# Attention output product for two heads' pairs at a time every second step, split a step later, and twenty narrower products of zeros

## The chip, the cores and the metric

The kernel runs on one core of a Trainium2 chip. The metric is the device time of one execution in microseconds (us). Engines are TensorE (PE, with its weight loads as PEld), VectorE (DVE), ScalarE (ACT), GpSimd (POOL) and SyncE (SP, which issues DMAs). Matmuls write into PSUM, eight banks of 512 fp32 columns by 128 partitions.

## The reference

Talking-heads attention (the heads are mixed before and after the softmax), then a dense gated MLP, then a routed mixture of experts. The change touches the attention alone:

```
batch, heads, seq, dim = 2, 12, 448, 64
scores = scale * q @ k.T                              # per batch and head
scores = einsum('bhij,hg->bgij', scores, w_pre)       # heads mixed
attn   = softmax(scores)
attn   = einsum('bhij,hg->bgij', attn, w_post)        # heads mixed again
x      = attn @ v                                     # -> [batch*seq, heads*dim]
x      = (x @ w_a) * (x @ w_b) @ w_out                # first MoE part, dense
out    = routed experts of x (8 experts, top 1)
```

All is fp32; the first dense product takes x as a sum of a rounded high part and a rest (hi and lo, `xh` and `xl`).

## The kernel before

The queries are cut into blocks of 120, 120, 120 and 90 per batch, eight blocks in all. A block is worked off in steps: `self.seq` lists 46 steps, n = 0 to 45, six for a block of 120 queries and five for one of 90. The order on every engine is the order of the code, written out by hand as a software pipeline in `Attention.run`. In step n TensorE does, in this order:

- `postmix` of step n - 1 into the two PSUM banks o (L165): the attention weights mixed over heads, transposed by the matmul. The exponentials `e` are the stationary operand.
- `qk_mm` (L90): the scores of one pair of heads of a later block, into the two banks s. The last are done in step 36.
- `premix` of step n + 2 (L122): the scores mixed over heads, into banks of the pool t. It has three banks; a step takes two, one for each r.
- `av` (L189): the output product attn @ v of the block before, one sixth of it (two heads, `p` = 0 to 5) at a time, into the single bank v. A sixth of a block of 120 takes 120 columns of the bank.

ScalarE has in a step: the exponentials of step n + 1 (L139), one half of the copy of o into `A2T` (L177), one half of the score copy into `S` (L96), and the high part of the output product, `xh` (L206). VectorE has the other half of the copy of o (L177), the normaliser (L147, L148), the other half of the score copy (L97), the row maxima of step n + 2 (L130), and the low part `xl`, which is the product minus its high part (L207). GpSimd scales the post-mix weights (L151) and issues most of the DMAs that rearrange the scores from `S` to `G` for `premix` (L111).

Sixths of a block become due in the second step of the block behind it. Before, a step takes one sixth, or two if there are more sixths left than steps. Of the last block all six sixths come behind the loop, in banks s and o. In the last steps a hook adds work: VectorE decodes weights for the dense part from step 39 on (L372 to L376), ScalarE and VectorE split them in step 42 (L392, L393), and steps 44 to 46 each end with six dense products (L414) behind everything else on TensorE.

Ahead of all this TensorE multiplies zeros (L233) while the first loads are under way.

Of the kernel before, what the change touches and what calls it, by code (L numbers as in the profile page):

```python
# [27 lines left out]
HP = H // 2  # L28
# [5 lines left out]
class Attention:  # L34
# [174 lines left out]
    def run(self, hook=None):  # L209
        nc = self.nc  # L210
        nb, N = len(self.blocks), len(self.seq)
        first = {}
        for n, s in enumerate(self.seq):
            first.setdefault(s[0], n)
        first[nb] = N
        AH, LAG, PRE = 5, 1, 5
        self.on_sp = [n < 10 or n - 1 in first.values() or n in first.values() for n in range(N)]
        c = self.c
        cs = self.att.tile([128, 4, 64], F32, name="cs")
        self.load_q(0)  # L220
        for p in range(HP):
            self.load_k(0, p)
        self.load_q(1)
        nc.sync.dma_start(cs, self.a["wmix"])
        nc.sync.dma_start(self.kc, self.a["kc"])
        self.load_v(0, 0)
        self.load_v(0, 1)
        z = self.att.tile([128, 2, S], F32, name="e", bufs=3)
        nc.vector.memset(z[:, 0, 0:256], 0.0)
        z = z[:, 0, 0:256].bitcast(BF16)  # L230
        zp = self.pair("t")
        for i in range(14):
            nc.tensor.matmul(zp[i % 2][:, :360], z[:, 0:128], z[:, :360], start=True, stop=True)  # L233
        nc.gpsimd.tensor_tensor(out=c["wpre"], in0=cs[:, 0], in1=cs[:, 1], op=ALU.mult)
        nc.gpsimd.tensor_scalar(out=c["wpre"], in0=c["wpre"], scalar1=0.125, scalar2=None, op0=ALU.mult)
        nc.gpsimd.tensor_tensor(out=c["wpost"], in0=cs[:, 2, 0:GK], in1=cs[:, 3, 0:GK], op=ALU.mult)
        for p in range(HP):
            self.qk_pair(0, p, ("s", "o", "tt", "tv")[p % 4])
        todo = [(blk, p) for blk in range(1, nb) for p in range(HP)]
        nrel = [0]  # L240
        def rel(n):
            while nrel[0] < min(n, N, first[todo[0][0]] if todo else N):
                self.relayout(nrel[0])
                nrel[0] += 1
        rel(2)
        self.load_q(2)
        rel(AH)
        for i in range(PRE):
            self.qk_pair(*todo.pop(0), "so"[i % 2])
        for m in range(2):  # L250
            self.premix(m)
            self.rowmax(m)
        self.exps(0)
        self.norm(0)
        loads = {}
        for i in range(HP):
            if i > 1:
                loads[i - 1] = lambda i=i: self.load_v(0, i)
            loads[9 + i] = lambda i=i: self.load_k(1, i)
            loads[(20, 22, 26, 27, 28, 29)[i]] = lambda i=i: self.load_v(1, i, True)  # L260
        parts = []
        for n in range(N + LAG):
            av, k = [], 0
            m = n - LAG
            if n < N:
                blk, g0, nr, last = self.seq[n]
                if n - 1 in first.values() and blk > 0:
                    parts = [(blk - 1, p) for p in range(HP)]
                left = (first[blk + 1] if blk + 1 < nb else N - 1) - n + 1
                av = [parts.pop(0) for _ in range(min(len(parts), 2 if len(parts) > left else 1))]  # L270
                if todo:
                    tb = todo[0][0]
                    need = sum(1 for x in todo if x[0] == tb)
                    if tb < 2 or n > first[tb - 1] - AH:
                        slots = first[tb] - AH - n + 1
                        k = min(need, 2 if need > slots else 1)
            if m >= 0:
                self.postmix(m)
            out = []
            for _ in range(k):  # L280
                for f in out:
                    f()
                out = [self.qk_mm(*todo.pop(0))]
            if n + 2 < N:
                self.premix(n + 2)
            if n + 1 < N:
                self.exps(n + 1)
            if m >= 0:
                self.a2t(m, 0)
                self.a2t(m, 1)  # L290
            if n + 1 < N:
                self.norm(n + 1)
            for f in out:
                f()
            pso = [(*av[0], len(av), self.av(*av[0], len(av)))] if av else []
            if n + 2 < N:
                self.rowmax(n + 2)
            for x in pso:
                self.av_out(*x)
            rel(n + 1 + AH)  # L300
            if n < N:
                for tb in range(3, nb):
                    if n == first[tb - 2] - 3:
                        self.load_q(tb)
                loads.get(n, lambda: None)()
            if not todo and not self.qk_closed:
                self.qk_es.close()
                self.qk_closed = True
            if self.qk_closed and nrel[0] == N and not self.s_closed:
                self.s_es.close()  # L310
                self.s_closed = True
            if hook:
                hook(n)
        self.last = nb - 1
# [1020 lines left out]
```

## Time and profile before

| | us |
|---|---|
| median of 3 runs | 627.27 |
| lowest and highest of them | 626.29, 630.08 |
| the profiled execution | 626.63 |
| its span, first to last instruction | 624.9 |
| TensorE busy with matmuls in it | 598.6 |
| VectorE busy | 416.1 |
| ScalarE busy | 234.0 |
| GpSimd busy | 143.4 |

The profile shows one execution. Its span is 1.73 us shorter than its time; what lies around the span is not seen. The attention loop runs to about 188 us of it; the dense part and the routed experts follow. Matmuls overlap, and the end of one is modelled, so the starts of TensorE's groups tell more than their busy time.

### The profile page before, as it was taken

How to read it: one execution, taken by the hardware profiler on the slowest of the kernel's cores; microseconds unless marked ns; L12 is line 12 of the kernel's file. 1: busy time of each engine (PE TensorE's matmuls, PEld its weight loads, DVE VectorE, ACT ScalarE, POOL GpSimd, SP SyncE). 2: the span in 40 equal slices, each digit the busy share in tenths (PEclk: the TensorE clock that was granted, in tenths of full speed). 3: DMA queues.
4: the chain of work that ended last, by engine and by line, in shares of the span. 5: the costliest groups of instructions: out<-in, count | busy, mean ns of one | idle time of the engine just before them, and what ended most of it. 6: DMA issues, size and time to landing. Idle time of an engine off the chain costs nothing. (4 is left out here: it accounts for less than half of the span.)

```text
span 624.9 us, 16865 instructions
## 1 busy us (share of the span) xinstructions
PE 598.6 (96%) x6843; PEld 497.7 (80%) x6843; DVE 416.1 (67%) x993; ACT 234.0 (37%) x544; POOL 143.4 (23%) x243
## 2 busy tenths in 40 slices
PE   8789999999999999999999999999999999979993
PEld 3346666666778999999999979999998888769982
DVE  4478787878856878777777555987759833593322
ACT  4376676766652211111111252212364222361221
POOL 3477666767700000000000015000100101101101
PEclk9799999999999999999999999999999999979998
DMA  7677638656322654444455003310490661156102
GB/s 225 177 193 189 187 114 206 177 180 171 119 64 72 231 188 167 152 152 160 171 178 201 0 1 116 140 50 26 175 335 1 252 254 53 48 225 259 48 31 66
DMA packets 38178, 89.89 MB, mean 144 GB/s; under 512 B 12208, under 2 KB 15596, under 8 KB 38076
## 3 DMA queue, kind: packets, MB, share of 16 engines
q1 hardware_dynamic: 24060, 64.60, 30.7%
q0 software_dynamic: 14016, 23.95, 13.0%
q8 instruction: 62, 1.02, 0.7%
q14 instruction: 40, 0.33, 0.2%
HBM read 69.88 MB, written 5.70 MB: 121 GB/s over the span
## 5 line engine op out<-in xcount | busy, mean ns | idle before, releaser
L111 POOL DMA_DIRECT2D G<-S x156 | 92.2, 609 | 18.9 <-issue 7.8
L1131 PE MATMUL y<-ra,gh 128*128 128x384 f32 x324 | 70.6, 340 | 0.0
L392 ACT CAST whi<-wdec 128x768 fp32r<-128x768 f32 x24 | 20.0, 835 | 124.2 <-DVE wdec L376 116.9
L139 ACT ACTIVATE e<-t,st 124x448 f32<-124x448 f32 x90 | 56.2, 633 | 15.1 <-DVE st L130 15.1
L838 PE MATMUL ph<-ra,xsh 128*128 128x512 f32 x168 | 54.9, 409 | 5.0 <-ACT ra L801 4.5
L130 DVE TENSOR_REDUCE st<-t 124x1 f32<-124x448 f32 x90 | 52.1, 619 | 11.2 <-PE t L122 8.4
L165 PEld LDWEIGHTS o<-Wp,e 60*56 60x56 f32 (+1 forms) x2880 | 48.2, 132 | 13.7 <-issue 12.5
L1131 PEld LDWEIGHTS y<-ra,gh 128*128 128x128 f32 x324 | 56.8, 188 | 0.6 <-issue 0.3
L122 PE MATMUL t<-G,wpre 60*64 60x448 f32 x360 | 53.4, 555 | 3.9 <-DMA G<-S 3.6
L165 PE MATMUL o<-Wp,e 60*56 60x60 f32 (+1 forms) x2880 | 54.0, 221 | 2.4 <-issue 1.4
L189 PEld LDWEIGHTS v<-A2T,vt 120*64 120x64 f32 x672 | 33.6, 136 | 26.6 <-DVE st L148 18.3
L1107 POOL TENSOR_TENSOR ra<-wo,ra 128x768 fp32r<-128x768 f32 x4 | 10.6, 2673 | 191.5 <-ACT ra L1106 191.5
L915 PE MATMUL py<-ra,gh 128*128 128x384 f32 x224 | 49.2, 342 | 0.0
L90 PE MATMUL s<-Kt,Q 64*64 64x448 f32 (+2 forms) x336 | 45.6, 551 | 0.6 <-ACT S L96 0.6
L807 POOL DMA_INDIRECT fa<-yd,idc x11 | 11.5, 1049 | 145.1 <-DVEq L874 64.3
L189 PE MATMUL v<-A2T,vt 120*64 120x120 f32 (+1 forms) x672 | 42.3, 269 | 0.2 <-DVE xl L207 0.2
L177 DVE COPY A2T<-o 120x480 f32<-120x480 f32 (+1 forms) x46 | 30.9, 671 | 16.0 <-PE o L165 15.8
L1131 PE MATMUL y<-ra,gl 128*128 128x384 f32 x162 | 41.3, 336 | 0.0
L838 PEld LDWEIGHTS ph<-ra,xsh 128*128 128x128 f32 x168 | 31.8, 195 | 11.6 <-ACT ra L801 4.9
L915 PEld LDWEIGHTS py<-ra,gh 128*128 128x128 f32 x224 | 38.8, 188 | 1.0 <-issue 1.0
L393 DVE TENSOR_TENSOR wlo<-wdec,whi 128x768 fp32r<-128x768 f32 x24 | 23.0, 958 | 22.4 <-ACT whi L392 22.3
L122 PEld LDWEIGHTS t<-G,wpre 60*64 60x64 f32 x360 | 20.6, 136 | 20.9 <-issue 6.4
(248 smaller groups left out, 1236.2 us busy)
## 6 DMA issues: line engine op xcount, KB each, us to landing
wraw<-in_wab_dram SPq DMA_DIRECT2D x48, 384.0 KB
G<-S POOLq DMA_DIRECT2D x156, 105.0 KB, 3.9
fa<-in_w_dram SPq DMA_DIRECT2D x4, 3072.0 KB
wor<-in_w_out_dram SPq DMA_DIRECT2D x12, 768.0 KB
r1f<-in_w_dram SPq DMA_DIRECT2D x2, 3072.0 KB
r1f<-in_wg_dram SPq DMA_DIRECT2D x8, 384.0 KB
r1f<-in_w_dram SPq DMA_DIRECT2D x4, 768.0 KB
fa<-in_w_dram SPq DMA_DIRECT2D x4, 768.0 KB
```

The lines of the kernel that those rows point to most:

```text
L90: nc.tensor.matmul(ps[r][64 * h:64 * h + m, :S], q[64 * r:64 * r + 64, p * 2 * hw + h * hw:p * 2 * hw + h * hw + m], k[64 * r:64 * r + 64, ...
L111: (self.nc.sync if r == 0 and (h == 0 and self.on_sp[n] or n < 2) else self.nc.gpsimd).dma_start(g[64 * r:64 * r + GK, h, :], self.S[blk][ ...
L122: nc.tensor.matmul(t[r][64 * h:64 * h + 64, :S], w[64 * r:64 * r + GK, :], g[64 * r:64 * r + GK, h, :], start=True, stop=True)
L130: self.nc.vector.tensor_reduce(out=st[:124, r:r + 1], in_=self.T[n][r][:124, :S], op=ALU.max, axis=AX.X, negate=True)
L139: self.nc.scalar.activation(e[:124, r, :], t[r][:124, :S], AF.Exp, bias=st[:124, r:r + 1], scale=1.0, accum_out=st[:124, 2 + r:3 + r])
L165: nc.tensor.matmul(o[h][64 * u:64 * u + m, c0:c0 + GK], e[64 * h:64 * h + GK, r, x:x + m], wp[64 * h:64 * h + GK, r, :], start=True, stop= ...
L177: (nc.scalar.copy if h == 0 else nc.vector.tensor_copy)(dst, src)
L189: nc.tensor.matmul(ps[u * 64:(u + 1) * 64, i * w:(i + 1) * w], self.vt[b, p][:, j, u, :], at[:, j * H + 2 * p + u, :w], start=(j == 0), st ...
L393: lambda: V.tensor_tensor(out=lo, in0=x3, in1=hi.bitcast(F32), op=ALU.subtract)]
L838: nc.tensor.matmul(ps, x[:, d], self.w1[:, hf, s, d], start=(d == 0 and i == 0), stop=(d == ND - 1 and i == 2))
L915: nc.tensor.matmul(y[q][:, :384], hx[:, f % 4], self.w2[:, f, s, q * 384:(q + 1) * 384], start=(f == 0 and i == 0), stop=(f == NFC - 1 and ...
L1131: nc.tensor.matmul(y[q][:, :384], gx[:, f % 6], wov[:, f, s, 384 * q:384 * (q + 1)], start=(t > 0 and f == 0 and i == 0), stop=(f == NF - ...
```

## The change

The sixths of a block go two by two into one bank, in the first, third and fifth of the steps in which one went before; the step between has no output product. The high and low part of such a pair are made in the step behind it, after that step's row maxima, except where another output product comes at once: then they are made ahead of that product. That happens twice: at step 24, since the block before has five steps, and at step 45, where the last two sixths are taken because it is the loop's last step; there its own pair is split at once too. Ahead of the loop, 14 products of zeros with 360 columns become 20 with 255.

```diff
-        for i in range(14):
-            nc.tensor.matmul(zp[i % 2][:, :360], z[:, 0:128], z[:, :360], start=True, stop=True)
+        for i in range(20):
+            nc.tensor.matmul(zp[i % 2][:, :255], z[:, 0:128], z[:, :255], start=True, stop=True)
...
-        parts = []
+        parts, pso = [], []
         for n in range(N + LAG):
...
                 if n - 1 in first.values() and blk > 0:
-                    parts = [(blk - 1, p) for p in range(HP)]
-                left = (first[blk + 1] if blk + 1 < nb else N - 1) - n + 1
-                av = [parts.pop(0) for _ in range(min(len(parts), 2 if len(parts) > left else 1))]
+                    parts, at = [(blk - 1, p) for p in range(HP)], n
+                if parts and ((n - at) % 2 == 0 or n == N - 1):
+                    av = [parts.pop(0) for _ in range(2)]
...
-            pso = [(*av[0], len(av), self.av(*av[0], len(av)))] if av else []
+            if av:
+                for x in pso:
+                    self.av_out(*x)
+                pso = []
+            done, pso = pso, ([(*av[0], len(av), self.av(*av[0], len(av)))] if av else [])
             if n + 2 < N:
                 self.rowmax(n + 2)
-            for x in pso:
+            for x in done + (pso if n >= N - 1 else []):
                 self.av_out(*x)
+            if n >= N - 1:
+                pso = []
```

On TensorE, at steps 7 and 8, where the output product of the first block begins (v is its bank, t that of the pre-mix, o that of the post-mix, s that of the scores; x8 are the eight matmuls of a sixth):

```order
 L90 MATMUL s<-Kt,Q 60x448
 L122 MATMUL t<-G,wpre 64x448 x4
-L189 MATMUL v<-A2T,vt 64x120 x8
+L189 MATMUL v<-A2T,vt 64x120 x16
 L165 MATMUL o<-Wp,e 64x60
 L165 MATMUL o<-Wp,e 56x60 x2
```

```order
 L90 MATMUL s<-Kt,Q 45x448
 L122 MATMUL t<-G,wpre 64x448 x4
-L189 MATMUL v<-A2T,vt 64x120 x8
 L165 MATMUL o<-Wp,e 64x60
 L165 MATMUL o<-Wp,e 56x60 x2
```

The second sixth has moved from step 8 into the group of step 7, and in step 8 the post-mix follows the pre-mix directly.

On ScalarE, from the copy of the weights of step 42 to the end of the loop (e are exponentials, A2T the copy of o, xh the high part). Before:

```order
L392 CAST whi_3263<-wdec 128x768
L139 ACTIVATE e,st<-t,st 124x448 x2
L177 COPY A2T<-o 120x2x48x5
L206 CAST xh<-v 128x2x12x10
L139 ACTIVATE e,st<-t,st 124x448
L177 COPY A2T<-o 120x2x48x5
L206 CAST xh<-v 128x12x10
L177 COPY A2T<-o 120x2x48x5
L206 CAST xh<-v 128x12x10
L177 COPY A2T<-o 120x48x5
```

Now:

```order
L398 CAST whi_3221<-wdec 128x768
L139 ACTIVATE e,st<-t,st 124x448 x2
L177 COPY A2T<-o 120x2x48x5
L206 CAST xh<-v 128x2x12x10
L139 ACTIVATE e,st<-t,st 124x448
L177 COPY A2T<-o 120x2x48x5 x2
L206 CAST xh<-v 128x2x12x10 x2
L177 COPY A2T<-o 120x48x5
```

The high part of the pair of step 44, the first of the two in the row with x2, now stands behind step 45's copy of o, and ahead of the high part of step 45's own pair.

## Rows read from the trace of the kernel before

**Rows 1.** Windows, three stretches of the loop: start:end, length, busy of each engine (instructions), clock, DMA

```profile
46.55:152.65 106.10, 105.34 (x2772) 70.34 (x2772) 85.08 (x205) 71.79 (x202) 73.69 (x145) 1.00 0.64 176
152.65:175.09 22.44, 22.44 (x642) 15.93 (x641) 19.54 (x47) 14.69 (x43) 14.79 (x27) 1.00 0.34 112
175.09:187.99 12.90, 12.68 (x311) 10.13 (x310) 6.14 (x14) 6.57 (x15) 0.67 (x2) 1.00 0.21 66
```

**Rows 2.** Waits from 46.55 to 152.65: total us, times, longest

```profile
ACT xh L206 <- PE v L189: 30.8, 28, 1.9
```

**Rows 3.** Timeline of PE, one steady step with one sixth: start, busy, instruction

```profile
64.82 1.10 PE L165 MATMUL o<-Wp,e 60*64 60x60 f32 x62
...
66.48 1.01 PE L122 MATMUL t<-G,wpre 60*64 60x448 f32 x8
67.42 1.04 PE L189 MATMUL v<-A2T,vt 120*64 120x120 f32 x16
68.39 1.10 PE L165 MATMUL o<-Wp,e 60*64 60x60 f32 x62
```

**Rows 4.** Timeline of PE, the step with two sixths, 19

```profile
94.15 1.86 PE L189 MATMUL v<-A2T,vt 120*64 120x120 f32 x32
95.94 0.37 PE L165 MATMUL o<-Wp,e 60*64 60x60 f32 x9
```

**Rows 5.** Timeline of PE, early steps without an output product

```profile
42.68 0.99 PE L122 MATMUL t<-G,wpre 60*64 60x448 f32 x8
43.43 1.09 PE L165 MATMUL o<-Wp,e 60*64 60x60 f32 x62
...
46.55 1.11 PE L165 MATMUL o<-Wp,e 60*64 60x60 f32 x63 [0.26 <-ACT A2T L177]
```

**Rows 6.** Timeline of all engines, the same steps

```profile
42.89 0.53 ACT L96 COPY S<-s 124x448 f32<-124x448 f32 x1
...
43.82 1.16 DVE L130 TENSOR_REDUCE st<-t 124x1 f32<-124x448 f32 x2 [0.17 <-PE t L122]
...
44.54 0.63 ACT L139 ACTIVATE e<-t,st 124x448 f32<-124x448 f32 x1 [1.12 <-DVE st L130]
...
47.43 0.63 ACT L139 ACTIVATE e<-t,st 124x448 f32<-124x448 f32 x1 [0.59 <-DVE st L130]
...
48.21 1.01 PE L122 MATMUL t<-G,wpre 60*64 60x448 f32 x8
```

**Rows 7.** Timeline of PE, a step without scores

```profile
165.13 1.16 PE L165 MATMUL o<-Wp,e 60*64 60x60 f32 x64
166.11 1.05 PE L122 MATMUL t<-G,wpre 60*64 60x448 f32 x8
```

**Rows 8.** Timeline of all engines, steps 44 and 45

```profile
178.82 0.60 ACT L206 CAST xh<-v 128x240 fp32r<-128x240 f32 x1 [0.62 <-PE v L189]
...
179.45 0.58 DVE L207 TENSOR_TENSOR xl<-v,xh 128x240 fp32r<-128x240 f32 x1 [0.65 <-ACT xh L206]
...
180.09 1.04 PE L189 MATMUL v<-A2T,vt 120*64 120x120 f32 x16 [0.22 <-DVE xl L207]
...
182.48 1.16 PE L165 MATMUL o<-Wp,e 60*64 60x60 f32 x64
...
183.57 1.04 PE L189 MATMUL v<-A2T,vt 120*64 120x120 f32 x16
183.69 0.64 ACT L177 COPY A2T<-o 120x480 f32<-120x480 f32 x1 [2.13 <-PE o L165]
```

**Rows 9.** Timeline of PE, its first groups: the zeros and the first score products

```profile
1.19 4.38 PE L233 MATMUL t<-e 128*128 128x360 bf16 x14 [1.19 <-DVE e L229]
5.50 0.98 PE L90 MATMUL s<-Kt,Q 64*64 64x448 f32 x8
```

**Rows 10.** Windows, the score products behind the zeros and what follows

```profile
5.43:14.00 8.57, 8.57 (x87) 3.52 (x89) 5.90 (x10) 5.32 (x10) 3.21 (x7) 1.00 0.71 231
14.00:22.50 8.50, 5.46 (x26) 1.34 (x22) 2.22 (x4) 1.99 (x6) 5.57 (x10) 1.00 0.90 203
```

## The prediction

> **What bounds the kernel now.** Read first the window table of the three stretches that the change reaches: steps 7 to 35 of the attention loop, steps 36 to 42 (no score products after step 36), and steps 43 to 46 [rows 1]. TensorE has a matmul in flight for 105.34 of 106.10, all of 22.44, and 12.68 of 12.90 us, at the full granted clock of 1.00; VectorE fills 80% of the first stretch and ScalarE 68%. Then the list of waits [rows 2]: in 28 of the 29 steps the hi copy on ScalarE waits for the output product, 30.8 us in all, up to 1.9 us each. That is the wait which the change takes away, and it stands on an engine that is not the bound, so by itself it is worth nothing.
>
> What TensorE's time is made of is read from the starts of its groups. I call them o (post-mix, L165), qk (scores, L90), t (pre-mix, L122) and v (output product, L189). A step takes 3.57 us from o to o: 1.66 for o and qk, 0.94 for t, 0.97 for v [rows 3]. With two sixths in one group v takes 1.79, not 1.94 [rows 4]. In a step without v, the next o starts 0.75 after t, not 0.94 [rows 5]. So a v group costs 0.97 and makes the t before it 0.19 longer: a step without v needs 1.66 + 0.75 = 2.41, one with two sixths 1.66 + 0.94 + 1.79 = 4.39, together 6.80 where two single steps need 7.14. Each group that disappears is worth up to 0.34 us.
>
> **The change part by part.**
>
> Products of zeros. Fourteen of 360 columns take 4.31 us from the first start to the first score product [rows 9], or 308 ns each. In proportion to the columns, 255 take 218 ns, and twenty take 4.36. The score products start right behind, so I add 0.05. Bounds: 0 if the loads of Kt end this wait anyway, 0.5 if a narrow product carries 25 ns more than its columns say (20 x 25 ns; no row shows one, so this end is a guess).
>
> Steps 7 to 35. Before, 28 steps with one sixth and step 19 with two; after, 15 pairs, at 7, 9 and so on to 23, then 24, 26, 28, 30, 32, 34. Fourteen groups fewer: 14 x 0.34 = -4.8.
>
> But a new wait appears. The pool of t has three banks and a step takes two, so the second half of t(n+2) gets the bank that the first exponential of step n+1 frees. That makes a ring: t starts, 1.14 later its row maximum starts (42.68 to 43.82), 0.72 later the exponential (44.54), and 0.78 after the start of an exponential the next t starts (47.43 to 48.21) [rows 5, 6]. The ring needs 2.64. TensorE now comes round in 3.57 and never meets it; from the t of a step without v to the t of the step after it would come round in 0.75 + 1.66 = 2.41. So it waits 0.23, once a pair: the pair costs 7.03, and only 0.11 of the 0.34 is left. Of the 15 pairs, the one of step 7 has no short step of this kind ahead, that of step 15 follows step 14 with its two score pairs, and that of 24 follows another pair: 12 x 0.23 = +2.8. Bounds: 0 if the ring is tighter than these rows say, and 3.12 for the whole short step [rows 5] if ScalarE and VectorE don't catch up in the long one.
>
> Step 24. Block 2 ends with a pair at 23, block 3 begins with one at 24, and there is one v bank, so the pair of 23 is split ahead of the product of 24. Its hi copy stands behind the score copy on ScalarE, which ends 0.74 after t starts (42.89 + 0.53 against 42.68) [rows 5, 6]; then 0.60 for the copy of 240 columns and 0.03 to the subtraction, 0.58 for that and 0.06 to the product [rows 8]. The v group starts 2.01 after t instead of 0.94: +1.1. VectorE's row maximum of that step queues behind the subtraction, and step 25 is short of v, so I see nobody late after it. The stretch: -4.8 + 2.8 + 1.1 = -0.9.
>
> Steps 36 to 42, 22.44 us now. Here o is followed by t after 0.98 [rows 7]. Step 36 still has qk: 4.39 + 0.23 = 4.62. Then three pairs (37 without v and 38 with it, and so on). From the t of the short step to the next t TensorE would need 0.75 + 0.98 = 1.73, the ring 2.64: it waits 0.91. From there to the next short step's t: 0.94 + 1.79 + 0.98 = 3.71. A pair is 6.35, three are 19.05, and the stretch 23.67: +1.2. Bounds: -1.7 without the ring (4.39 + 3 x 5.44 = 20.71), and +2 if the decoding of weights, which shares VectorE from step 39 on, delays the row maximum.
>
> Steps 43 to 46, 12.90 us now with v in 43 (two), 44 and 45 (one each); after, two in 44 and two in 45. One group fewer, -0.3; step 44 comes sooner after 43, and its o may wait for the copy out of the o banks as in the short step, 0.26 [rows 5]. Step 45 has a pair right behind a pair again. The hi copy of 44 stands behind step 45's own copy of o on ScalarE. From the start of o: 1.21 to that copy (182.48 to 183.69), 0.64 for it, 0.60 + 0.03 for the hi copy, 0.58 + 0.06 for the subtraction: v starts at 3.12, where it now starts at 1.09 [rows 8]. TensorE has nothing else ahead of it in its queue, since the first MoE products are issued behind v: +2.0. Bounds: +1.4 if the hi copy follows closer than these durations, +2.3. Sum of the tail +1.9.
>
> The split on ScalarE and VectorE gets cheaper (one copy of 240 columns for two of 120), which nobody waits for. The output product needs V's last sixths no earlier than before: they are loaded at steps 26 to 29 and used from 32 on. SP's and GpSimd's queues are not touched.
>
> Sum: 0.05 - 0.9 + 1.2 + 1.9 = +2.2 us on the profiled execution of 626.63, which makes 628.9; that execution lies 0.64 below the median of the three runs, 627.27. I forecast **629.0**. One per cent, 6.3 us, is about what a measurement of this kernel can tell from no change; the forecast lies inside.
>
> **The rivals.**
>
> The ring does not bind and TensorE keeps what it saves. For it: the ring's distances come from the early steps, where ScalarE and VectorE are late, and may shrink when these have time. Against it: between them the engines did nothing else that could go. Then 0.05 - 4.8 + 1.1 - 1.7 + 1.9 = -3.5, or 623.2. The page TensorEngine Tiling (Array Packing) of the Trainium skill, under Key Properties, says that a change of tiling mode drains TensorE; v alone uses all 128 rows, so by that rule every group removed saves two drains, which the 0.94 against 0.75 agrees with, and it gives the sum just made, since nothing in it limits the gain.
>
> The copies out of PSUM become the bound, the slower side. A step without v takes the 3.12 that it takes in the early loop, where o waits for ScalarE's copy [rows 5], and the long step gives nothing back: 7.51 a pair against 7.14, 14 x 0.37 = +5.2, with 0.05, 1.1, 1.2 and 1.9 as before +9.4, or 636. It decides once ScalarE or VectorE have more than 6.8 us of work in two steps; the shares above give VectorE 5.7 and ScalarE 4.8 of 7.14 [rows 1], so it should not. The same page, under PSUM Bottleneck, warns that tiling speeds up TensorE but not the copying out of PSUM; in this trace the copies have 20% to spare.
>
> The clock comes later because the zeros are narrower. The 8.57 us from 5.43 on are all busy at 1.00 [rows 10]; at the lower level of 1.2 GHz they would take twice that. The wait for G behind them hides some 3 us (5.46 busy of 8.50), so up to +5.5 beside the sum, 634.4.
>
> The pair waits at 24 and 45 are covered, and the ring eats the rest: -0.9 - 1.1 + 1.2 - 0.3, about 625.6. Against it: the queue order of ScalarE leaves no way round.
>
> **How the numbers follow.** The forecast's case, 627 to 631.5, gets 0.56; the gain kept 0.17; the covered waits 0.12; the copies as a bound 0.11; the late clock 0.04. To leave out no more than 2 in 10 the range takes in most of the two faster cases and the slower edge of the forecast with its upper bounds: 624.0 to 633.5. Faster by over 1% means below 621.0, which needs the full gain and no tail: 0.03. Slower by over 1% is above 633.5: most of the copies' case and half of the clock's, 0.10. Within 1%: 0.87.
>
> **What would show it.** In the profile after: groups of 32 v records every second step; short steps of 2.4 and long ones of 4.6 in the main stretch, with t or its weight load waiting for ScalarE's exponential by some 0.2 in the long ones and 0.9 without scores; TensorE idle about 1 us at step 24 and 2 us at step 45, both ended by the subtraction. The waits of the hi copy for v fall from 30.8 to near nothing. Short steps of 3 us would show the copies as the bound; no wait for the exponentials, the gain kept; score products of 0.75 us stretched to 1.5 after the zeros, the late clock.

## The result and the profile after

The changed kernel takes **632.59 us** (median of 9 runs, 630.13 to 634.40); the kernel before, run beside it, 627.32 (9 runs, 626.29 to 630.08). The ratio is 1.0082, with a 95% interval of 1.0061 to 1.0104: 5.3 us slower by the medians and 5.1 by the ratio, whose middle, though not the end of its interval, lies inside one per cent. The forecast was +1.7 us against the median of before. The profiled execution after took 632.62 us with a span of 630.8, 6.0 more than before; the working had +2.2.

The windows of the changed kernel: the three stretches of [rows 1], then two short pieces of step 45. Columns are start:end, length, busy of PE, PEld, DVE, ACT, POOL with counts, the granted clock, DMA share and GB/s.

```profile
46.04:153.65 107.61, 104.91 (x2780) 74.08 (x2778) 79.45 (x189) 76.09 (x189) 72.96 (x145) 1.00 0.61 173
153.65:177.72 24.07, 22.89 (x644) 15.56 (x637) 19.74 (x46) 16.84 (x43) 14.94 (x28) 1.00 0.37 113
177.72:194.12 16.40, 14.28 (x313) 11.66 (x311) 6.15 (x14) 5.63 (x13) 0.67 (x2) 0.90 0.16 50
185.35:187.26 1.91, 0.01 (x1) 0.03 (x1) 1.26 (x2) 1.10 (x2) 0.00 (x0) 0.99 0.00 0
187.26:190.62 3.36, 3.35 (x32) 3.09 (x32) 0.00 (x0) 0.00 (x0) 0.00 (x0) 0.50 0.02 5
```

Against [rows 1]: steps 7 to 35 take 1.51 us more (forecast -0.9), steps 36 to 42 1.63 more (+1.2), steps 43 to 46 3.50 more (+1.9). Step 7 begins 0.51 earlier, and what follows 194.12 takes 436.72 in place of 436.86. So the whole loss lies in the three stretches of the change. TensorE is a hair less busy in the first (104.91 for 105.34) and idle for 2.70 us in place of 0.76; VectorE has 5.6 us less work.

The wait that the change was to take away is gone. The list of ScalarE's waits from 45 to 155 us has no wait of the hi copy any more, where [rows 2] has 30.8 us. What ScalarE waits for now:

```profile
ACT e L139 <- DVE st L130: 19.8, 28, 1.2
ACT A2T L177 <- PE o L165: 7.3, 12, 1.6
```

A steady pair, steps 16 and 17, on TensorE's timeline (start, busy, instruction), then what VectorE and ScalarE do between the two groups t:

```profile
83.00 1.00 PE L122 MATMUL t<-G,wpre 60*64 60x448 f32 x8
83.75 1.12 PE L165 MATMUL o<-Wp,e 60*56 60x60 f32 x62
...
85.50 1.14 PE L122 MATMUL t<-G,wpre 60*64 60x448 f32 x8
86.57 1.86 PE L189 MATMUL v<-A2T,vt 120*64 120x120 f32 x32
88.36 1.10 PE L165 MATMUL o<-Wp,e 60*64 60x60 f32 x62
```

```profile
84.17 1.16 DVE L130 TENSOR_REDUCE st<-t 124x1 f32<-124x448 f32 x2
```

```profile
84.89 0.63 ACT L139 ACTIVATE e<-t,st 124x448 f32<-124x448 f32 x1 [0.59 <-DVE st L130]
```

The short step ends 0.75 after its t and takes 2.42 from o to o, the long one (83.75 to 88.36) 4.61: the forecast had 2.41 and 4.62. In the long step t lasts 1.07, not 0.94, and its row maximum and exponential follow the t before by 1.17 and 0.72, the distances of [rows 6]. In these pairs the profile names no wait for the exponential: that the ring holds them is read from the distances alone.

The pairs without scores are as forecast too, here steps 39 and 40 on TensorE (matmuls, then the weight loads of the second t):

```profile
166.12 0.94 PE L122 MATMUL t<-G,wpre 60*64 60x448 f32 x6
167.13 1.16 PE L165 MATMUL o<-Wp,e 60*64 60x60 f32 x63
...
168.46 1.24 PE L122 MATMUL t<-G,wpre 60*64 60x448 f32 x7
169.64 1.86 PE L189 MATMUL v<-A2T,vt 120*64 120x120 f32 x32
171.43 0.58 PE L165 MATMUL o<-Wp,e 60*64 60x60 f32 x25
```

```profile
168.73 0.20 PEld L122 LDWEIGHTS t<-G,wpre 60*64 60x64 f32 x6 [0.51 <-ACT e L139]
```

From the o of one pair (165.14) to that of the next (171.43) are 6.29 us, forecast 6.35; the second t waits for the first exponential.

Step 45 on TensorE, ScalarE and VectorE, to be held against [rows 8]:

```profile
184.20 1.16 PE L165 MATMUL o<-Wp,e 60*64 60x60 f32 x64
187.26 3.47 PE L189 MATMUL v<-A2T,vt 120*64 120x120 f32 x32 [1.91 <-DVE xl L207]
190.66 0.47 PE L420 MATMUL t<-xh,whi 128*128 128x448 f32 x1
```

```profile
185.41 0.63 ACT L177 COPY A2T<-o 120x480 f32<-120x480 f32 x1 [3.61 <-PE o L165]
185.94 0.57 ACT L206 CAST xh<-v 128x240 fp32r<-128x240 f32 x1
```

```profile
186.54 0.57 DVE L207 TENSOR_TENSOR xl<-v,xh 128x240 fp32r<-128x240 f32 x1 [0.41 <-ACT xh L206]
```

The queue is the forecast one (copy of o, hi copy, subtraction, product), and v starts 3.06 after o, forecast 3.12. What was not forecast stands in the last of the windows: right behind the idle 1.91 us the granted clock is at 0.50, the level of 1.2 GHz, until 190.62, and the 32 products take 3.40 us where a pair takes 1.79.

### The profile page after: what moved, and what is told of

The parts are those of the page before. It is cut to its first block, busy times and chain, and to the rows that moved or that the text cites. A ratio compares the mean times of both kernels' runs of the same rounds, so it can differ in the third digit from the quotient of the medians.

```text
span 630.8 us, 16838 instructions
## 1 busy us (share of the span) xinstructions
PE 599.7 (95%) x6849; PEld 503.2 (80%) x6849; DVE 410.8 (65%) x975; ACT 239.3 (38%) x526; POOL 142.4 (23%) x243
## 5 line engine op out<-in xcount | busy, mean ns | idle before, releaser
L165 PEld LDWEIGHTS o<-Wp,e 60*56 60x56 f32 (+1 forms) x2880 | 51.9, 132 | 18.1 <-issue 16.0
L122 PE MATMUL t<-G,wpre 60*64 60x448 f32 x360 | 57.6, 557 | 4.6 <-DMA G<-S 4.2
L165 PE MATMUL o<-Wp,e 60*56 60x60 f32 (+1 forms) x2880 | 55.3, 220 | 2.5 <-issue 1.4
L1113 POOL TENSOR_TENSOR ra<-wo,ra 128x768 fp32r<-128x768 f32 x4 | 10.6, 2669 | 196.6 <-ACT ra L1112 196.6
L177 DVE COPY A2T<-o 120x480 f32<-120x480 f32 (+1 forms) x46 | 30.8, 669 | 29.8 <-PE o L165 29.8
L189 PE MATMUL v<-A2T,vt 120*64 120x120 f32 (+1 forms) x672 | 39.5, 272 | 3.1 <-DVE xl L207 2.9
L399 DVE TENSOR_TENSOR wlo<-wdec,whi 128x768 fp32r<-128x768 f32 x24 | 23.0, 958 | 22.3 <-ACT whi L398 22.3
```

Of the source, the lines that this page charges most:

```text
L122: nc.tensor.matmul(t[r][64 * h:64 * h + 64, :S], w[64 * r:64 * r + GK, :], g[64 * r:64 * r + GK, h, :], start=True, stop=True)
L165: nc.tensor.matmul(o[h][64 * u:64 * u + m, c0:c0 + GK], e[64 * h:64 * h + GK, r, x:x + m], wp[64 * h:64 * h + GK, r, :], start=True, stop= ...
L177: (nc.scalar.copy if h == 0 else nc.vector.tensor_copy)(dst, src)
L189: nc.tensor.matmul(ps[u * 64:(u + 1) * 64, i * w:(i + 1) * w], self.vt[b, p][:, j, u, :], at[:, j * H + 2 * p + u, :w], start=(j == 0), st ...
L399: lambda: V.tensor_tensor(out=lo, in0=x3, in1=hi.bitcast(F32), op=ALU.subtract)]
```

## The experiments

Each was timed against the kernel before in its own set of runs (medians of before there 628.0 to 628.8 us). The stretches are read from the starts of the groups o in each profile, the last to the first of the final output products.

| kernel | median us | before beside it | ratio, 95% interval | steps 7-35 | 36-42 | 43-46 |
|---|---|---|---|---|---|---|
| before | | 627.32 | | 106.10 | 22.44 | 12.90 |
| changed | 632.59 | 627.32 | 1.0061 to 1.0104 | 107.61 | 24.07 | 16.40 |
| e1_zeros | 629.23 | 628.28 | 0.9997 to 1.0032 | 106.55 | 22.02 | 12.90 |
| e2_attention | 638.91 | 628.28 | 1.0144 to 1.0203 | 107.56 | 23.50 | 14.78 |
| e7_no_max_after | 634.78 | 628.28 | 1.0078 to 1.0143 | 109.20 | 23.49 | 16.41 |
| e8_no_max_before | 630.15 | 628.28 | 0.9995 to 1.0043 | 105.87 | 22.40 | 12.87 |
| e3_tail_old | 631.71 | 628.82 | 1.0023 to 1.0062 | 108.33 | 23.50 | 12.86 |
| e4_scores_only | 631.56 | 628.82 | 1.0017 to 1.0057 | 107.71 | 22.25 | 12.90 |
| e5_no_queue | 629.45 | 628.82 | 0.9991 to 1.0037 | 107.51 | 22.99 | 12.97 |
| e6_split_at_once | 633.50 | 628.82 | 1.0037 to 1.0085 | 106.71 | 24.93 | 13.88 |
| e9_ring_after | 635.99 | 628.03 | 1.0091 to 1.0170 | 109.13 | 23.49 | 16.38 |
| e10_ring_before | 629.79 | 628.03 | 1.0000 to 1.0049 | 106.63 | 22.29 | 12.86 |
| e11_zeros_count | 633.68 | 628.03 | 1.0059 to 1.0116 | 107.65 | 23.50 | 14.78 |
| e12_split_ahead | 629.60 | 628.03 | 1.0004 to 1.0052 | 107.41 | 23.50 | 12.80 |

The theory at the start: the loss lies in two waits for a split that is queued late (steps 24 and 45, the second with a fall of the clock), in the ring t, row maximum, exponential, bank, and nowhere else. The rivals: the copies out of PSUM set the steps; the narrower zeros delay the clock; TensorE's stalls without a cause in the profile belong to merged groups.

**e1_zeros** is the kernel before with the new products of zeros alone.

```
-        for i in range(14):
-            nc.tensor.matmul(zp[i % 2][:, :360], z[:, 0:128], z[:, :360], ...)
+        for i in range(20):
+            nc.tensor.matmul(zp[i % 2][:, :255], z[:, 0:128], z[:, :255], ...)
```

> The kernel before with only the twenty products of zeros of 255 columns in place of the fourteen of 360; the attention loop is untouched. My theory (the loss lies in waits of the attention loop): the time of the kernel before within 0.5 us, 626.8 to 627.8, and the first output product of the loop's step of 27.08 us starts within 0.3 us of that. Rival, the narrower zeros raise the clock later: the granted clock rises at about 6.3 us instead of 5.43 and the time is 0.9 us or more above the kernel before.

Measured +0.9 us, with an interval from -0.2 to +2.0: neither side is excluded by the time. The profiles decide against the rival: the first o starts at 27.08, 28.37, 27.79 and 26.14 in the four profiles with fourteen products (before, e2, e8, e10) and at 27.71 in this one; in the changed kernel's it was 27.96. The 0.88 us at the start of that one are within this scatter: over all nine profiles with the narrow products alone the first o starts at 25.87 to 28.42.

**e2_attention** is the other half: the changed attention with the old zeros (the same lines, turned round).

> The changed kernel with the fourteen old products of zeros of 360 columns; the attention loop is the changed one. My theory: the whole loss but some tenths stays, 632 to 633, with the stretches of steps 7 to 35, 36 to 42 and 43 to 46 as in the changed kernel within 0.3 us each. Rival, the zeros carry 0.9 us of it: 631.7 or less. If TensorE's short stalls that no semaphore explains, of which the profile after has more than the one before, belong to the merged groups, this trace has them in the same number, 7 or so; if they are chance, their number and places differ.

It was neither: 10.6 us slower than before, 5 more than with the new zeros. The first stretch is that of the changed kernel, the second lacks one pair that was 0.58 dearer there (steps 37 and 38), and in the last, where the same wait of 1.91 us stands, the clock stays up, so it takes 14.78 and not 16.40. The excess lies 330 us later, in the expert part, at a branch. First the one branch in the changed kernel, then in this run (duration in ns, three times), then TensorE's next instruction in this run, and the window behind it:

```profile
L997 PEldq COMPARE_BRANCH  x1: 681/681/681, 524.4 to 524.4; - x1
```

```profile
L997 PEldq COMPARE_BRANCH  x1: 4577/4577/4577, 523.5 to 523.5; - x1
```

```profile
528.16 1.22 PE L844 MATMUL ph<-ra,xsh 128*128 128x512 f32 x2 [2.88 <-issue]
```

```profile
528.16:531.25 3.09, 3.09 (x7) 2.48 (x8) 0.49 (x3) 0.00 (x0) 0.00 (x0) 0.50 0.35 133
```

TensorE's sequencer needs 4.58 us for a branch that took 0.68, the engine runs out of work for 2.88, and the clock falls behind that. The two programs differ only in the products of zeros in front of everything: six fewer here, with their weight loads, and each wider.

**e11_zeros_count** restores the number of instructions and keeps the wide zeros.

```
         for i in range(20):
-            nc.tensor.matmul(zp[i % 2][:, :255], z[:, 0:128], z[:, :255], ...)
+            nc.tensor.matmul(zp[i % 2][:, :360 if i < 14 else 8], z[:, 0:128], z[:, :360 if i < 14 else 8], ...)
```

> The changed kernel with fourteen products of zeros of 360 columns and six of 8 columns: the old work in the new number of instructions. The run with the fourteen alone was 5 to 6 us slower than the changed kernel, and in its profile 2.88 us of that are one stall of TensorE at a branch in the expert part, where the same branch took 4.58 us in place of 0.68. My theory, the place of the code behind the branch decides: with the number of instructions restored the branch costs 0.7 to 2.1 us again and the time is 632 to 633.5, as the changed kernel. Rival, the wider zeros themselves cost it: 637 or more, as the run with the fourteen.

It is at +5.65 us, with the branch at

```profile
L997 PEldq COMPARE_BRANCH  x1: 2244/2244/2244, 524.5 to 524.5; - x1
```

So six tiny products give 5 us back, and the rival falls: not the width but the count matters. That it acts through the branch is read from one profile of each: in the other twelve kernels' profiles the same branch takes 0.68 to 2.58 us, and e2 alone has 4.58. That it is the place of the code behind the branch fits, but how the sequencer fetches it no run shows.

**e3_tail_old** and **e4_scores_only** hand out the sixths of the last queued block (e4: of the last two, `in (5, 6)`) by the old rule and split them at once.

```
+                old = bool(parts) and parts[0][0] in (6,)
+                if old:
+                    left = (first[blk + 1] if blk + 1 < nb else N - 1) - n + 1
+                    av = [parts.pop(0) for _ in range(min(len(parts), 2 if len(parts) > left else 1))]
-                if parts and ((n - at) % 2 == 0 or n == N - 1):
+                elif parts and ((n - at) % 2 == 0 or n == N - 1):
...
-            for x in done + (pso if n >= N - 1 else []):
+            for x in done + (pso if n >= N - 1 or old else []):
                 self.av_out(*x)
-            if n >= N - 1:
+            if n >= N - 1 or old:
                 pso = []
```

> The changed kernel with the sixths of the last queued block handed out by the old rule (two, two, one, one at steps 42 to 45) and split at once, so that no pair stands right behind a pair at step 45. My theory (the wait at step 45 and the fall of the granted clock in it cost 3.5 us together): steps 43 to 46 take 12.9 us again, the clock stays at 1.00 up to the final output products, and the time is about 629, 3.5 below the changed kernel. Rival, the loss of the tail belongs to the lower clock by chance and only the wait of 2 us goes: 630.6.

> The changed kernel with the sixths of the last two queued blocks by the old rule and split at once, so that pairs stand only beside steps that have score products. My theory: the 3.5 us of the tail and the 1.6 us of the pairs without scores (a ring of 2.64 us against 1.73 of work) go, 627.5 in all, with steps 36 to 42 at 22.4 us. Rival, the copies out of PSUM are the bound in every short step: the stretch of steps 36 to 42 falls, but by no more than 0.5 us.

Windows of e3 and of e4, the two last stretches each:

```profile
154.51:178.01 23.50, 23.27 (x645) 15.56 (x637) 19.67 (x46) 15.83 (x41) 15.12 (x28) 1.00 0.36 114
178.01:190.87 12.86, 12.65 (x312) 10.13 (x311) 6.35 (x15) 6.56 (x15) 0.67 (x2) 1.00 0.21 64
```

```profile
156.07:178.32 22.25, 22.25 (x644) 15.72 (x637) 20.35 (x49) 15.08 (x44) 15.58 (x28) 1.00 0.38 121
178.32:191.22 12.90, 12.69 (x313) 10.14 (x311) 6.16 (x15) 6.56 (x15) 0.67 (x2) 1.00 0.21 64
```

Each stretch does what the theory said: the tail is back at 12.9 with the clock up, and without the pairs steps 36 to 42 take 1.25 us less. In the whole time the tail is worth 2.4 us (the ratio falls by 0.0039, and the intervals just touch), less than the 3.5 of the theory and near the rival's 2, which had the clock fall by chance. The profiles bear that out: among the five profiles with the wait of step 45 it fell in three (changed, e7, e9: 16.4) and stayed in two (e2, e11: 14.78). The second step is not seen in the whole time (631.71 and 631.56, for 627.5 expected); 1.25 us is less than these intervals tell.

**e5_no_queue** takes a third block to the old rule as well (`in (2, 5, 6)`). The expectation means the block of step 24, but this is the one before it: the pairs of steps 21 and 23 are dissolved, so that none stands right ahead of step 24, and those of 24, 26 and 28 stay.

> As the run with the last two queued blocks by the old rule, and the block whose first pair at step 24 stood right behind the pair of step 23 by the old rule as well; pairs are left only in steps 7 to 23 and 30 to 35. My theory: the wait of about 1 us at step 24 goes and the gain of four merged pairs with it, 626.4 to 627.3 in all, equal to the kernel before within 1 us. Rival, merged groups gain nothing anywhere or lose by TensorE's unexplained stalls: steps 7 to 35 take 107 us or more, and the time is 628 or above.

It equals the kernel before within 1 us (+0.6 to +0.9, with an interval from -0.6 to +2.3), as the theory said; but steps 7 to 35 take 107.51 and the time is over 628, as the rival said. Step 24 is at 3.99 in place of 5.10, and dearer steps elsewhere eat it (step 26 5.85, 32 5.48). What pairs are left gain nothing in this profile.

**e6_split_at_once** splits every pair in its own step.

```
-            for x in done + (pso if n >= N - 1 else []):
+            for x in pso:
                 self.av_out(*x)
-            if n >= N - 1:
-                pso = []
+            pso = []
```

> The changed kernel with each pair split into hi and lo in its own step and not a step later. My theory: the two waits for the subtraction, at steps 24 and 45, go (about 1.1 and 2 us, with 1.6 of the clock), but the copies of 240 columns now stand behind the product in the long step and make the next short step's copy of o and exponential late, so steps 36 to 42 lose up to 1 us more: 629 to 631. Rival, the lateness of the split is the whole loss: 627 or less.

The two waits go (steps 22 to 25 take 14.36 in place of 15.1 to 16.2 in the five profiles of the changed code, steps 43 to 46 13.88), but the time is no better, +3.8 us by the ratio and +4.7 by the medians: steps 36 to 42 lose 1.4 more, and this list of TensorE's waits from 150 to 200 us says why:

```profile
PE o L165 <- ACT A2T L177: 2.1, 4, 1.4
```

With the hi copy ahead of the exponential the next o waits for the copy out of its banks. So the rival falls, and so does my 629 to 631: splitting late is right in general and wrong ahead of another pair.

**e12_split_ahead** follows from that: only a pair with a pair in the next step is split at once.

```
-            for x in done + (pso if n >= N - 1 else []):
+            now = n >= N - 2 or n in first.values()
+            for x in done + (pso if now else []):
                 self.av_out(*x)
-            if n >= N - 1:
+            if now:
                 pso = []
```

> The changed kernel with a pair split in its own step where the next step holds a pair too (the steps ahead of 24 and of 45); all other pairs are split a step later as in the change. My theory (what the two waits cost is the place of the split in the queues, not the pair): step 24 falls from 5.10 to about 4.1 us, steps 43 to 46 from 14.8 to 16.4 to about 13, the clock stays at 1.00 there, and the time is 628 to 630. Rival, two pairs in adjacent steps cost as such, by the one v bank or by the copies: 631 or above.

629.60, +1.6 us against before: 3.4 us of the loss by the ratios, 3.7 by the medians, are gone. Step 24 takes 3.99. Step 45 and its window:

```profile
185.00 1.16 PE L165 MATMUL o<-Wp,e 60*64 60x60 f32 x64
186.09 1.86 PE L189 MATMUL v<-A2T,vt 120*64 120x120 f32 x32
```

```profile
178.53:191.33 12.80, 12.59 (x313) 10.17 (x311) 6.17 (x14) 5.76 (x13) 0.67 (x2) 1.00 0.22 64
```

v starts 1.09 after o, as in [rows 8], though pairs still stand in adjacent steps. That the place of the split in the queues causes these two waits is shown.

**e7_no_max_after, e8_no_max_before, e9_ring_after, e10_ring_before** were to cut the row maximum out of the ring, in the changed kernel and as a control in the one before. All compute the maximum and leave it out of the exponent.

```
+            self.nc.scalar.activation(e[:124, r, :], t[r][:124, :S], AF.Exp, bias=self.zb[:124], scale=1.0,
+                                      accum_out=sm[:124, r:r + 1])
```

(e9 and e10; e7 and e8 keep `accum_out=st[:124, 2 + r:3 + r]`.)

> The changed kernel with the exponential's bias a tile of zeros: the row maximum is still computed and is left out of the exponent, so that the exponential no longer waits for VectorE's maximum. My theory (a ring of t, row maximum, exponential, bank): the ring shortens by the maximum, 0.7 us, so the long steps lose their wait, 4.62 to about 4.40, and a pair without scores falls from 6.29 to about 5.6; over the twelve pairs of steps 7 to 35 and the three of steps 36 to 42 some 2.5 + 2 us, 628 in all. Rival, the copies out of PSUM and the work on ScalarE set the steps: the times of the steps stay within 0.1 us, and the total within 1 us of the changed kernel's.

> The control for the run on the changed kernel: the kernel before with the exponential's bias a tile of zeros; the row maximum is still computed and is left out of the exponent. My theory: TensorE comes round in 3.57 us and does not meet the ring, so the main stretch stays at 106.1 within 0.3 us and the total within 0.5 us of the kernel before. Rival, the maximum delays TensorE in the kernel before too: over 1 us faster.

> The changed kernel with the exponential cut off from VectorE: its bias is a tile of zeros and its sums go to a tile of their own, so that it shares no tile with the row maximum; the maximum is computed and left out of the exponent. The first try shared the tile of sums and still waited for the maximum, in 15 to 16 waits of the same length. My theory (a ring of t, row maximum, exponential, bank): the exponential starts right behind t, the long steps fall from 4.62 to about 4.40 us and the dearer ones (steps 9, 13, 21, 23, 26, 30, 32) too, and a pair without scores from 6.29 to about 5.6: steps 7 to 35 take 104 to 105.5 in place of some 107.8, steps 36 to 42 about 21.5 in place of 23.5. Rival, ScalarE's queue of copies sets the steps: less than 0.5 us in either stretch.

> The control: the kernel before with the exponential cut off from VectorE in the same way, the row maximum computed and left out of the exponent. My theory: TensorE never met the ring in that kernel, so steps 7 to 35 stay at 106.2 within 0.4 us and steps 36 to 42 at 22.3 within 0.4. Rival: both stretches gain as much as in the changed kernel, and then the ring is not what the merged groups met.

Both tries failed to cut the link (in e7 too there were 35 such waits; the 15 to 16 of the text above were miscounted). ScalarE's waits from 46 to 178 us in the changed kernel and in e9:

```profile
ACT e L139 <- DVE st L130: 24.8, 35, 1.3
```

```profile
ACT e L140 <- DVE st L130: 23.3, 34, 1.2
```

The exponential still starts behind the maximum of the same bank t, and steps 36 to 42 stay at 23.49. So these runs say nothing on the ring with or without the maximum; that the maximum is part of it rests on the traces' distances alone. The controls agree with the kernel before within 0.6 us in every stretch, but with the link uncut they control nothing. That e7 and e9 are slower than the changed kernel by their medians (intervals overlap) was not followed up.

## Why the prediction was right in its kind and wrong in its size

It forecast no gain, a small loss and where it lies; the time after lies in its range, but of the +6.0 us in the span it had +2.2. What it lacks is 2.4 us in steps 7 to 35, 0.4 in steps 36 to 42 and 1.6 in the tail, less 0.7 outside the stretches. That 632.59 is still in the range is in part luck: its slower edge, 633.5, took in bounds that were not reached (0.5 for the zeros, short steps of 3.12, 2 us for the decoding of weights), while the clock behind the wait of step 45, 1.6 us, had none. And 629.0 is not quite its own sum, which puts the median at 627.27 + 2.2, or 629.5.

- **Zeros, +0.05.** Right by themselves as far as e1 can tell. Not seen: their number matters 330 us later, by 5 us between e2 and e11.
- **Steps 7 to 35, -0.9: the step that failed, by 2.4 us.** The size was off, not the mechanism. Steps 11, 17, 19 and 34 take 4.61 to 4.62, as worked out. (The 0.78 from an exponential to the next t was read where t starts 1.66 after its o, as it does in a steady step without a wait; the trace after has it where a wait is named, 54.85 to 55.63 in step 9.) But "it waits 0.23, once a pair" took the ring of a steady step for all. Over five profiles with the same code here (changed, e2, e3, e4, e11) the smallest times are 4.92 in step 9, 4.65 in step 15 (4.39 due), 5.03 in step 23 (where o has half the products, so 4.19 was due), 4.70 in step 26 (4.22 due, with 90 queries) and 4.82 in step 32: 2.1 us more together. In steps 9, 26 and 32 of the changed kernel the row maximum starts 1.39 to 1.49 after its t, not 1.17, because VectorE's score copy ahead of it waits for a DMA that still reads `S`; in these steps of the kernel before it does not wait. Step 9, where that t starts at 52.65 and the exponential at 54.85, on VectorE and among TensorE's weight loads:

```profile
53.60 0.62 DVE L97 COPY S<-s 109x448 f32<-109x448 f32 x1 [0.43 <-DMA G<-S]
54.14 1.15 DVE L130 TENSOR_REDUCE st<-t 124x1 f32<-124x448 f32 x2
```

```profile
55.63 0.20 PEld L122 LDWEIGHTS t<-G,wpre 60*64 60x64 f32 x6 [0.33 <-ACT e L139]
```

Step 15 meets the ring although step 14 has two score pairs, because these stand ahead of the t at which the ring begins. In step 23 of the changed kernel the t before starts at 103.88 and TensorE comes round 0.43 sooner than in a full step, which the ring does not; the weight load of t then waits three times as long as forecast:

```profile
106.76 0.41 PEld L122 LDWEIGHTS t<-G,wpre 60*64 60x64 f32 x6 [0.70 <-ACT e L139]
```

The ring of that step is 2.88 (103.88 to 106.76), not 2.64. Two other long steps are no case of it: step 21 (4.81) follows a short step of 2.00, whose t has half the products, and in step 30 (4.95 or more) the scores start late behind a stall without a semaphore, as they do in the kernel before (4.22 in place of 3.57). What is left of the 2.4 is the balance of such stalls.
- **Step 24, +1.1.** Right: 5.10 in four of those profiles, 3.99 in e12. In the profile after it is 5.81; 0.71 of that is a stall of TensorE in o that no semaphore explains and that the four others lack.
- **Steps 36 to 42, +1.2.** Right: 23.49 or 23.50 in six profiles, 1.2 more than the mean of 22.3 of those with single sixths (before, e1, e8, e10). The profile after had one dearer pair (0.6).
- **Steps 43 to 46, +1.9.** Right without the clock: 14.78. The clock behind the wait adds 1.6 when it falls. The prediction priced the wait, and not that an engine that has been idle may come back at half speed.
- **The rivals.** The ring binds, so 623.2 was out. The Trainium skill (TensorEngine Tiling (Array Packing), Key Properties) says that a change of tiling mode drains TensorE. The short step of 2.42 agrees with that rule; what it saves is waited for a step later. Short steps of 3.1 us were not seen, so the copies are not the bound in the changed kernel; in e6 they become it at four places. The late clock: the first stretch at a granted clock of 1.00 did begin later in the profile after, at 6.30 in place of 5.43, but nothing says that the zeros did it. Over the nine profiles with the narrow products alone it begins at 4.01 to 7.10, over the four with the wide ones alone at 4.29 to 6.60. The waits at 24 and 45 were not covered.

Open stays what TensorE's short stalls without a semaphore are. The kernel before has them too (in e1 step 10 takes 4.43 us in place of 3.57, step 26 4.03 in place of 3.37), so they are not the merged groups' own. In profiles of the same code they change place: step 24 in the changed kernel, 10 in e3, 30 in e2.

## What to carry to other kernels

A wait that is removed from an engine off the bound gives nothing; merging groups on the bound gives at most what a group costs beyond its products (0.34 us here), and only until the next ring closes: work out the ring for the irregular steps (half-filled ones, block edges, steps in which an engine of the ring waits for a DMA), not for the steady one alone. Where work is put off by a step, look for the places at which the next user of its buffer comes right behind, and flush early there and only there. An edit at the front of a long program can change the time of a later branch by microseconds: compare the parts behind the edit before the whole time is put down to it.

## What was not expected of the hardware

- One branch of TensorE's sequencer (line 991 of before, 997 of the changed kernel) took 0.68, 0.80, 2.20, 2.24 and 4.58 us in the changed kernel, e1, before, e11 and e2, and 1.16 to 2.58 us in the nine other kernels. In e2 it left TensorE idle for 2.88 us, and all six runs of that kernel took 637.0 to 641.5 us.
- An idle time of 1.91 us behind over 145 us at the full clock was followed by 3.4 us at a granted clock of 0.50 in three profiles, and by none in two profiles of the same code there.
- The exponential on ScalarE waits for the row maximum on VectorE although they share only the PSUM bank that both read (34 waits, 23.3 us in e9). The profile shows a semaphore; whether the chip needs that order, or the program was merely built with it, no run shows.
